# Thirty-eight more idle matmuls ahead of two waits of TensorE

## The chip, the cores and the metric

The kernel runs on one core of one Trainium2 chip. The metric is the time of the whole program in device microseconds (us), as the median of several runs. One further execution was recorded by the hardware profiler; all traces and rows below are of that one execution, and their times count from its first instruction (its span).

The engines are called by short names: PE is TensorE (matmuls; PEld is its weight load), DVE is VectorE, ACT is ScalarE, POOL is GpSimd, and SP is the queue that issues most DMA transfers.

## What is computed

A gated linear recurrence over 768 steps for 4 batches and 8 heads of width 48 is followed by a two-layer network with the SiLU function on the 3072 rows of width 384 that come out of it:

```python
    f = 1.0 / (1.0 + np.exp(-f_logit))
    for t in range(S):
        state = f[:, :, t, :, None] * state + np.einsum('bhd,bhe->bhde', k[:, :, t], v[:, :, t])
        y[:, :, t] = np.einsum('bhd,bhde->bhe', q[:, :, t], state)
    ...
    h = x @ w_in
    g = h * (1.0 / (1.0 + np.exp(-h)))
    return (g @ w_out).astype(np.float32)
```

Here x is y with the heads side by side, w_in is 384 x 2048 and w_out is 2048 x 384.

## The kernel before

**Units.** The 768 steps are cut into 6 chunks of 128, and one chunk of one batch, with all 8 heads, is a unit: 24 units, and two neighbours make a pair. Within a unit the recurrence is done in matrix form. ACT makes the logs of the gates (E and L in the plan, lines 492 and 494); PE sums them along the chunk with a triangular matrix (cs, L565 and L569); ACT takes exponentials of the sums; POOL scales k (ki, L578) and DVE scales q (qg, L582). PE transposes both (tq, L588) and DVE copies them out (L590). PE multiplies them to scores (sc, L599), DVE masks these (at, L603), and PE makes y from scores, v and the carried state (y, L608 and L612). DVE casts y (yc, L616), PE transposes it (yT, L620), and DVE copies it to xT (xc, L622). PE also makes the unit's own contribution to the state (d, L630), which DVE adds (sd, L635 or L637) and POOL scales (su, L641).

**The network.** PE multiplies the columns of w_in with xT (m1, L529, one unit at a time for the first six units: 12 matmuls for each quarter of w_in; mi, L540, for pairs later), ACT applies SiLU into hT (L526, L536), and PE multiplies by w_out (mo, L551). DVE copies the result out and it is stored.

**Weights.** w_in and w_out arrive as four loads each into staging buffers (L505, L510) and are cast to bf16, a quarter at a time (ci and co in the plan, L518 to L520). The four casts of w_in are on POOL, POOL, POOL and DVE; the fourth quarter's, on DVE, is ci 3. In the plan's order PE uses the quarters 1, 2, 3 and then 0. Quarter 0 of w_in is cast by POOL.

**What sets the order.** A planner at build time (`make_tasks`, `schedule`, `planned`) writes every step down as a task with an engine, a duration, a rank, the tasks that it depends on and the buffers that it takes. It simulates the program once, and the order of tasks on each engine is then fixed; at run time each engine goes through its own list and waits on semaphores. SP's list holds the loads, so a load that waits for a buffer holds back all that is behind it.

PE's list in the stretch that matters is: yT of unit 1; cs of unit 3, which waits for the logs of unit 3; sc of unit 2; m1 of units 0, 1 and 0 (36 matmuls in all); y of unit 2; m1 of unit 1; then m1 of unit 0 with quarter 3, which waits for ci 3; yT of unit 2; m1 of unit 1 with quarter 3; d of unit 2; m1 of unit 2; tq of unit 3; m1 of units 0 and 1 with quarter 0; sc of unit 3; three more m1 of unit 2; and then mo.

**Idle matmuls.** `idle` (L386) looks through PE's plan up to 60 us for gaps. In each it finds the accumulator bank that is free for longest, and counts how many matmuls fill `idle_fill` of that stretch, at 0.0565 us each (0.113 for the first gap). The program then issues that many matmuls of a zero tile (`blank`, 128 x 128) into the bank just before the task that ends the gap; nothing reads their results (`warm`, L650 to L652, called at L672). The planner does not count their time. In the kernel before there are nine such groups, of 21, 23, 15, 18, 4, 18, 5, 6 and 2 matmuls. The group of 6 stands ahead of cs of unit 3, and the group of 2 ahead of m1 of unit 0 with quarter 3.

Of the kernel before, what the change touches and what calls it, by code (L numbers as in the profile page):

```python
# [38 lines left out]
    idle_to=60.0,  # L39
    idle_gap=0.2,  # L40
    idle_fill=0.75,
    hold_exp=0,
    hold_silu=1.23,
    keep_exp=161.0,
# [331 lines left out]
def planned(cfg, slots):  # L376

    tasks, T = make_tasks(cfg)
    schedule(tasks, slots, cfg, cfg["margin"])
    fixed = {e: sorted([t for t in tasks if t.eng == e], key=lambda t: (t.start, t.idx)) for e in ENGINES}  # L380
    schedule(tasks, slots, cfg, 0.0, fixed=fixed)
    order = sorted(tasks, key=lambda t: (t.start, t.idx))
    return order, idle(order, slots, cfg)


def idle(order, slots, cfg):  # L386

    held = {s: [] for s in range(slots["mlp"])}
    banks = {}
    for t in order:  # L390
        for x in t.acq + t.use:
            if x.cls == "mlp":
                lo, hi = banks.get(x, (t.start, t.end))
                banks[x] = (min(lo, t.start), max(hi, t.end))
    for x, (lo, hi) in banks.items():
        held[x.slot].append((lo, hi + 0.3))
    out, prev = [], cfg["idle_from"]
    for t in [t for t in order if t.eng == "PE"]:
        lo, hi = prev, t.start - cfg["idle_gap"]
        prev = t.start + t.dur  # L400
        if t.start > cfg["idle_to"]:
            break
        best = (0.0, 0.0, 0)
        for s, spans in held.items():
            a = max([lo] + [e for b, e in spans if b < hi])
            if hi - a > best[0] + 1e-6:
                best = (hi - a, a, s)
        n = int(best[0] * cfg["idle_fill"] / (0.0565 if out else 0.113))
        if n > 0:
            out.append((best[1], best[2], n))  # L410
    return out
# [296 lines left out]
```

## Time and profile before

| what | value |
|---|---|
| median of 4 runs | 189.99 us (188.86 to 190.88) |
| the profiled execution's own time | 191.16 us |
| its span, first to last instruction | 189.4 us |
| mean granted TensorE clock in it | 0.98 of full |
| PE busy | 176.1 us, 93% of the span |
| ACT busy | 131.2 us, 69% |
| DVE busy | 95.9 us, 51% |
| POOL busy | 70.4 us, 37% |
| idle matmuls (L652) | 112 |

The profiled execution is one sample, and its time is not the median's. The busy shares are means over the whole span. PE is busy nearly throughout, except in the opening: its waits there are for the first logs, for the logs of unit 3 and for the cast of the last-used but one quarter of w_in. A granted clock of 1.00 is full speed, 0.50 is half. In a row of the timeline the first number is the start, the second the length, "xN" the number of instructions merged, and the bracket gives the engine's idle time before the row and what ended it. Rows of PE overlap a little, because a matmul is recorded until its result is written (0.219 us for one of 128 columns) while the next has long begun.

### The profile page before, as it was taken

What the parts mean: (1) busy time and instruction counts of PE and PEld (TensorE: products, weight loads), DVE (VectorE), ACT (ScalarE), POOL (GpSimd) and SP (SyncE); (2) the same over time, 40 slices, a digit from 0 to 9 for tenths busy, and PEclk for the clock granted to TensorE, in tenths of its full rate; (3) what the DMA queues carried; (4) which work ended last, traced back from release to release, by engine and by line L of the source; (5) the groups of instructions that cost most, each with busy time, mean ns of one, the idle gap of its engine ahead of it and who ended that gap; (6) DMA issues with size and microseconds to landing.
All of it is one profiled execution on the core that took longest, in us unless ns stands there. A gap on an engine that the chain in (4) does not pass through costs nothing.

```text
span 189.4 us, 4875 instructions
## 1 busy us (share of the span) xinstructions
PE 176.1 (93%) x2005; PEld 141.6 (75%) x2005; DVE 95.9 (51%) x185; ACT 131.2 (69%) x217; POOL 70.4 (37%) x112
## 2 busy tenths in 40 slices
PE   5985669999999999979999999999999999999991
PEld 4974559877787879778787787668788786966960
DVE  4286244346768793473625736875651515251111
ACT  4460743798797898998988798468669996720720
POOL 2344636734555752382570750581152106000000
PEclk9999786999999999999999999999999999999999
DMA  6999999899999999999999489469785775413101
GB/s 120 203 182 279 393 302 360 214 238 234 191 251 197 246 228 212 208 245 188 195 155 248 100 163 225 88 115 214 144 169 130 158 146 114 121 24 104 42 11 72
DMA packets 120389, 34.22 MB, mean 181 GB/s; under 512 B 116128, under 2 KB 117792, under 8 KB 120368
## 3 DMA queue, kind: packets, MB, share of 16 engines
q1 hardware_dynamic: 119664, 31.76, 77.4%
q0 software_dynamic: 704, 2.16, 3.1%
q8 instruction: 15, 0.25, 0.5%
q14 instruction: 6, 0.05, 0.1%
HBM read 25.17 MB, written 4.72 MB: 158 GB/s over the span
## 4 chain that ended last, share of the span: by engine, by line
PE 77%; SPq 8%; DMA 6%; ACT 5%; issue 1%; DVE 1%; ACTq 0%; DVEq 0%
PE mlp L551 31%; PE mlp L540 24%; PE mlp L529 8%; SPq L485 6%; DMA ws<-in_moe_w_in_dram 6%; PE sc L599 3%; PE yd L612 2%; PE yd L608 2%; PE tq L588 2%; PE cs L565 2%; PE yd L630 2%; ACT L677 2%; PE tq L620 1%; ACT hT L536 1%; ACT e L492 1%
## 5 line engine op out<-in xcount | busy, mean ns | idle before, releaser
L551 PE MATMUL mlp<-w_out,hT 128*128 128x384 bf16 x384 | 69.9, 326 | 0.0
L536 ACT ACTIVATE hT<-mlp 128x512 bf16<-128x512 f32 x72 | 41.7, 597 | 17.4 <-PE mlp L540 14.9
L540 PE MATMUL mlp<-xT,w_in 128*128 128x256 bf16 x432 | 51.5, 273 | 1.1 <-ACT hT L536 1.0
L551 PEld LDWEIGHTS <-hT 128*128 128x128 bf16 x384 | 34.8, 97 | 19.5
L540 PEld LDWEIGHTS <-w_in 128*128 128x128 bf16 x432 | 46.3, 114 | 3.2 <-issue 1.3
L578 POOL TENSOR_TENSOR qk<-k,ia 128x384 bf16<-128x384 f32 x24 | 24.0, 999 | 51.7 <-ACT al L576 30.1
L603 DVE TENSOR_TENSOR atm<-sc,triu 128x512 bf16<-128x512 f32 x48 | 30.9, 685 | 21.0 <-PE sc L599 21.0
L677 ACT ACT_TABLE_LOAD x23 | 29.5, 1283 | 0.4
L641 POOL TENSOR_TENSOR st<-sd,al 48x192 bf16<-48x192 f32 x40 | 20.9, 522 | 17.2 <-DVE sd L635 8.7
L529 PE MATMUL mlp<-xT,w_in 128*128 128x128 bf16 x288 | 21.5, 238 | 1.9 <-DVE w_in L520 1.9
L529 PEld LDWEIGHTS <-w_in 128*128 128x128 bf16 x288 | 19.7, 120 | 2.5 <-DVE w_in L520 2.0
L559 DVE COPY o<-mlp 128x384 f32<-128x384 f32 x22 | 12.2, 556 | 18.2 <-PE mlp L551 14.5
L616 DVE CAST yb<-yd 128x384 bf16<-128x384 f32 x24 | 13.3, 554 | 15.9 <-PE yd L612 15.8
L572 ACT ACTIVATE ia<-cs 128x384 f32<-128x384 f32 x24 | 11.7, 489 | 13.7 <-PE cs L569 7.6
L582 DVE TENSOR_TENSOR qk<-q,cs 128x384 bf16<-128x384 f32 x24 | 13.2, 551 | 11.7 <-ACT cs L574 8.4
L526 ACT ACTIVATE hT<-mlp 128x512 bf16<-128x512 f32 x24 | 13.6, 597 | 7.8 <-PE mlp L529 7.4
L492 ACT ACTIVATE e<-f 128x768 f32<-128x768 f32 (+1 forms) x14 | 10.5, 747 | 8.7 <-DMA f<-in_f_logit_dram 8.7
L580 POOL CAST vb<-v 128x384 bf16<-128x384 f32 x24 | 11.6, 503 | 10.6 <-DMA v<-in_v_dram 7.6
L635 DVE TENSOR_TENSOR sd<-yd,st 128x384 f32<-128x384 f32 x16 | 8.9, 555 | 8.3 <-PE yd L630 6.2
L565 PE MATMUL cs<-lf,triu 128*128 128x384 bf16 x24 | 8.0, 332 | 4.5 <-ACT lf L494 4.5
L574 ACT ACTIVATE cs<-cs 128x384 f32<-128x384 f32 x24 | 11.4, 477 | 0.6
L652 PE MATMUL mlp<-blank 128*128 128x128 bf16 x112 | 10.0, 256 | 1.0 <-DVE blank L657 1.0
(43 smaller groups left out, 151.5 us busy)
## 6 DMA issues: line engine op xcount, KB each, us to landing
f<-in_f_logit_dram SPq DMA_DIRECT2D x10, 384.0 KB, 5.8
k<-in_k_dram SPq DMA_DIRECT2D x10, 384.0 KB, 5.8
q<-in_q_dram SPq DMA_DIRECT2D x10, 384.0 KB, 6.1
v<-in_v_dram SPq DMA_DIRECT2D x10, 384.0 KB, 5.3
ws<-in_moe_w_in_dram SPq DMA_DIRECT2D x4, 768.0 KB, 9.5
wt<-in_moe_w_out_dram SPq DMA_DIRECT2D x4, 768.0 KB, 8.1
out_dram<-o SPq DMA_DIRECT2D x13, 192.0 KB, 2.1
out_dram<-o POOLq DMA_DIRECT2D x11, 192.0 KB, 3.9
```

The lines of the kernel that those rows point to most:

```text
L492: nc.scalar.activation(e, at("f", u // 2)[:, i:i + n], AF.Exp, scale=-1.0)
L526: return nc.scalar.activation(at("hT", P)[:, 4 * j:4 * j + 4, i * C:(i + 1) * C], h, AF.Silu)
L529: nc.tensor.matmul(h[:, r, :], w_tile(kk, 4 * j + r), at("xT", P)[:, kk, i * C:(i + 1) * C], start=(kk == 0), stop=(kk == KT - 1))
L536: return nc.scalar.activation(at("hT", P)[:, 2 * j:2 * j + 2, :], h, AF.Silu)
L540: nc.tensor.matmul(h[:, i, :], w_tile(kk, n), at("xT", P)[:, kk, :], start=(kk == 0), stop=(kk == KT - 1))
L551: nc.tensor.matmul(o, at("hT", P)[:, n, i * C:(i + 1) * C], w_rows(n), start=(n % (NT // 2 if half else NT) == 0), stop=(n == NT - 1 or ha ...
L578: nc.gpsimd.tensor_mul(at("qk", u)[:, 1, :, 0:D], at("k", P)[:, i], at("ia", u))
L582: nc.vector.tensor_mul(at("qk", u)[:, 0, :, 0:D], at("q", P)[:, i], at("cs", u)[:, 0:HD].rearrange("p (h d) -> p h d", d=D))
L603: nc.vector.tensor_mul(at("atm", u)[:, r], at("sc", u)[:, r], triu[:, None, :].to_broadcast([C, NP, C]))
L616: nc.vector.tensor_copy(at("yb", u), at("y", u))
L641: nc.gpsimd.tensor_mul(at("st", u)[lo:lo + D, :, r * D:(r + 1) * D], at("sd", u)[lo:lo + D, :, r * D:(r + 1) * D], at("al", u)[lo:lo + D, ...
L677: nc.scalar.preload_act_table_set(SETS[after[t.idx]])
```

## The change

Two groups get more idle matmuls: the one ahead of the task `cs` of unit 3 gets 14 more (20 in place of 6), and the one ahead of the task `m1` of unit 0 with quarter 3 gets 24 more (26 in place of 2). Names of tasks are joined with underscores to look the numbers up. All else, the order on every engine included, stays.

```diff
@@ -39,6 +39,7 @@
     idle_to=60.0,
     idle_gap=0.2,
     idle_fill=0.75,
+    idle_more={'cs_3': 14, 'm1_0_3': 24},
     hold_exp=0,
     hold_silu=1.23,
     keep_exp=161.0,
@@ -406,6 +407,7 @@
             if hi - a > best[0] + 1e-6:
                 best = (hi - a, a, s)
         n = int(best[0] * cfg["idle_fill"] / (0.0565 if out else 0.113))
+        n += cfg["idle_more"].get("_".join(map(str, t.name)), 0) if n else 0
         if n > 0:
             out.append((best[1], best[2], n))
     return out
```

## The prediction

> **What bounds the kernel now.** I read the chain of work that ended last first, because a change on TensorE (PE) pays only where PE is on it. In order of time (start, length, what) it is this around the two places that the change touches:
>
> ```profile
> 15.93 11.04 DMA ws<-in_moe_w_in_dram
> 27.00 0.97 DVE w_in L520
> 28.01 1.35 PE mlp L529 x12
> 29.36 0.32 PE tq L620 x3
> 29.68 1.28 PE mlp L529 x12
> ```
>
> Up to 28.01 us the end is set by a load of w_in and its cast on VectorE (DVE); the first wait, cs of unit 3 at 20.68, is not on the chain. From 28.01 on it is nearly all PE, and the waits of PE from 31 to 186 us come to 1.0 us in all. So time saved on PE before 28.01 is lost again in the wait for the cast; time saved after 28.01 can reach the end. The timeline of PE shows both waits, the idle time in brackets:
>
> ```profile
> 17.12 0.50 PE L652 MATMUL mlp<-blank 128*128 128x128 bf16 x6
> 20.68 0.32 PE L565 MATMUL cs<-lf,triu 128*128 128x384 bf16 x1 [3.06 <-ACT lf L494]
> ...
> 21.34 3.82 PE L529 MATMUL mlp<-xT,w_in 128*128 128x128 bf16 x36
> ...
> 25.88 0.28 PE L652 MATMUL mlp<-blank 128*128 128x128 bf16 x2
> 28.01 1.35 PE L529 MATMUL mlp<-xT,w_in 128*128 128x128 bf16 x12 [1.86 <-DVE w_in L520]
> ...
> 34.22 2.20 PE L529 MATMUL mlp<-xT,w_in 128*128 128x128 bf16 x36
> ```
>
> The 36 matmuls after the first wait take 3.82 us, the same 36 at 34.22 take 2.20. The reason is the clock. I laid windows over the stretch from where the half-us windows change from 1.00 to 0.50 and back (the columns are stretch, length, PE busy with its count, granted clock, DMA share, GB/s):
>
> ```profile
> 14.55:17.96 3.41, 2.44 (x39) 1.00 0.95 276
> 17.96:21.38 3.42, 0.70 (x14) 1.00 1.07 391
> 21.38:24.79 3.41, 3.41 (x35) 0.50 1.08 370
> 24.79:28.20 3.41, 1.55 (x31) 1.00 1.04 293
> 28.20:31.62 3.42, 3.42 (x37) 0.50 0.99 380
> 31.62:35.03 3.41, 3.41 (x63) 1.00 1.05 244
> ```
>
> Twice a stretch of 3.41 us in which PE was little busy (0.70 us, then 1.55 us, 45%) is followed by one at half clock. A stretch with 2.44 us (71%) is followed by full clock. The second half-clock stretch, 28.20 to 31.62, lies on the chain.
>
> **The change part by part.** It adds 38 matmuls of zeros (with 38 weight loads, overlapped) and no wait, transfer or work on another engine. Each is costed from the rows of L652: 18 in 1.18 us at 9.66 us, of which the last takes its full 0.219, so (1.18 - 0.219)/17 = 0.0565 us each at full clock; 21 in 2.42 us at 0.99 us, of which the last takes some 0.31, so 2.11/20 = 0.106 us each at half.
>
> First wait, 14 more: 14 x 0.0565 = 0.79 us, so that the run of 20 ends near 18.4 instead of 17.62. At half clock, 20 x 0.106 = 2.1 us ends at 19.3. Both are hidden by the wait for the logs, which ends at 20.68; cost on the path 0. Cover gone, it would cost 0.79. What it buys: busy time in 17.96 to 21.38 rises from 0.70 to about 1.15 us, 34%. That is under the 45% after which the clock fell, so I expect the half clock from 21.38 to stay. Did it go, PE would reach the second wait about 1.7 us earlier and wait for the cast that much longer: worth nothing by itself.
>
> Second wait, 24 more: 24 x 0.0565 = 1.36 us, because the clock row says 1.00 from 24.79 on. The 26 end near 27.5 and the matmuls of unit 0 behind them start at 28.01 when the cast is done, as before: 0.5 us to spare, cost 0. The other bound is half clock, 25.88 + 26 x 0.106 = 28.64, a delay of 0.63 us; I take 0, since nothing in that stretch ran at half. What it buys: busy time in 24.79 to 28.20 becomes 1.55 + 1.36 = 2.91 us, 85%, above the 71% that kept full clock. So 28.20 to 31.62 should be at full clock.
>
> **Worked out at full clock** (12 matmuls of L529 = 12 x (2.20 - 0.22)/35 = 0.68 us; transposes and d 0.17 each, as their rows in the chain after 39 us have it): m1 of unit 0 from 28.01 to 28.69, yT of unit 2 to 28.86, m1 of unit 1 to 29.54, d to 29.71, m1 of unit 2 to 30.39. Its input xT is ready: the yT that ends at about 29.02 with its tail is copied by DVE in 0.36 us, by 29.41. Next come the transposes tq of unit 3, and here a load is late next:
>
> ```profile
> 30.45 0.56 DVE L582 TENSOR_TENSOR qk<-q,cs 128x384 bf16<-128x384 f32 x1 [0.38 <-DMA q<-in_q_dram]
> ```
>
> That product waits for q of unit 3 until 30.45, not for PE, ends at 31.01, and tq can start at about 31.08. It started at 32.01. So 0.93 us is gained of some 1.6, and 0.7 becomes a wait for q. The next, m1 of unit 0 with the cast on GpSimd (POOL) that ends at 29.72 + 1.46 = 31.18, is ready when tq is done at 31.53.
>
> The gain then has to pass unit 4's q, whose load is queued on SP behind a load of w_out:
>
> ```profile
> 34.65 0.34 SPq L510 DMA_DIRECT2D wt<-in_moe_w_out_dram  x1
> 35.03 1.37 SPq L485 DMA_DIRECT2D k<-in_k_dram  x1
> 36.45 2.67 SPq L485 DMA_DIRECT2D q<-in_q_dram  x1
> ```
>
> ```profile
> 42.87 0.55 DVE L582 TENSOR_TENSOR qk<-q,cs 128x384 bf16<-128x384 f32 x1 [2.25 <-DMA q<-in_q_dram]
> ```
>
> The w_out load waits for a buffer that a POOL cast frees, which follows the state update of unit 2, which follows DVE's sd at 31.37. With PE early, sd comes right behind the product that ends at 31.01, so this train moves 0.35 us at most. The product at 42.87 then ends between 43.07 (the load comes 0.35 earlier) and 43.42 (it lands as before), tq of unit 4 can start 0.07 later, and it started at 43.88: gain left 0.74 or 0.39, by the share of the DMA engines (1.16 on average from 40 to 50 us) rather between them. I take 0.6. Behind it PE waits for no q until 91.75 us, where DVE waited 0.24 for one, and one v at 136 us came late by 7.6 us on POOL without stopping PE; I charge nothing for these, and lower the end of the range for them.
>
> **Sum for the profiled execution:** 0 + 0 - 0.6, a span of 189.4 to about 188.8, and 191.16 to 190.56 in its own time. That execution lies 1.17 above the median of the runs, 189.99, and above the highest, 190.88. It may be one that met both half-clock stretches where others did not.
>
> **A rule that speaks against the change.** TensorE: Matmul & The Clock Gate (its sections on the clock gate and on why it matters) says that the clock drops after an idle window of about 3.4 us, and gives as a rule that only gaps over about 3 us matter. By that rule the second wait, 1.86 us, does no harm and the sum is 0: 189.99. The trace shows half clock after it, so I go by the trace. The same page (section What's actually happening) says that the window runs free and does not start with the kernel; one trace can't show that. If so, the boundaries lie elsewhere in each execution, and the gain of 0.6 belongs only to those where the second wait fills one window. I estimate that most but not all do, and move the median by 0.5.
>
> **Rivals.**
> - *Nothing changes*: 190.0. The median execution has no half clock after 28, or the gain is held up at the late loads of q. For it: 189.99 against 191.16, and the two waits for q. Against it: PE waits only 1.0 us behind 31.
> - *Slower, by the first 14*: if a window's boundary falls into the middle of the first wait, 2.3 us of idle time split in two may no longer lower the clock. Then PE is at full clock at 21.34, reaches the second wait some 1.7 us earlier, at about 24.2, finishes its 26 blanks at 25.7, and idles 2.3 us until 28.01: more than the 1.86 that sufficed. The half clock then comes after 28 in executions that before came to the second wait late and did not have it. Price 0.4 to 0.93, so 190.4 to 190.9. It decides once the boundaries lie about 0.9 to 1.4 us later than in this trace. Against it: with the boundaries of this trace it does not happen.
> - *The blanks are too long*: a cast done 0.5 us earlier than here, or half clock under the blanks, makes them delay unit 0's matmuls by up to 0.63: 190.6 without a gain, but full clock follows and pays that back. I count it into the one before.
>
> **How the numbers follow.** Gain of 0.3 to 1.0 at the median (189.0 to 189.7): 0.5. Nothing: 0.3, at 189.99 and 0.4 to each side, since four runs spread over 2.02. Slower: 0.2, 190.3 to 191.2. The likeliest gives 189.99 - 0.5 = 189.5; its own range is 188.9 to 189.8. For eight times in ten I leave out a tenth at each side: 188.6 to 190.8. A measurement of this kernel tells about 1% from no change, which is 1.9 us here: more than the whole half-clock stretch can cost (1.7). So faster by over 1% has 0.08, which only scatter of the runs adds; slower by over 1% has 0.05; within 1% 0.87.
>
> **What would show it.** Right: 20 and 26 blanks before the two waits, the first wait at about 2.3 us and the second at 0.5, half clock still once near 21 to 25 but full clock from 28 to 32, tq of unit 3 near 31.1 behind a wait of some 0.7 for q, tq of unit 4 near 43.3. Wrong in the step on the clock: a stretch at 0.50 behind 28 all the same. Wrong in the step on the loads: full clock there, and unit 4's tq at 43.5 or later. Wrong in cost: m1 of unit 0 later than the cast's end plus 0.05. A change of over 1.9 us would mean that something other than these two waits has moved.

## The result, and the profile after

The changed kernel takes 189.82 us (median of 36 runs), the kernel before 189.93 (55 runs). The ratio of the two times, changed over before, is 1.0002, with a 95% interval of 0.9989 to 1.0014: no change, within a quarter of a microsecond. Runs in a slower state, here one of the 36 at 194.04 us, are left out of every ratio. The profiled execution of the changed kernel took 190.72 us, its span is 188.95.

The clock did what the change can make it do. In the page of the changed kernel the row of the granted clock, in 40 slices of the span, is never below nine tenths:

```profile
PEclk9999999999999999999999999999999999999999
```

The row says nothing of the opening: the trace records the clock only from its first rise, here at 10.56 us, and the idle matmuls ahead of that go at half pace (23 in 2.61 us).

The timeline of PE around the two waits (lines are two higher after the change: L567 is cs, L531 m1, L590 tq, L654 the idle matmuls, called blanks below):

```profile
18.31 1.28 PE L654 MATMUL mlp<-blank 128*128 128x128 bf16 x20
19.90 0.32 PE L567 MATMUL cs<-lf,triu 128*128 128x384 bf16 x1 [0.31 <-ACT lf L496]
...
24.35 1.61 PE L654 MATMUL mlp<-blank 128*128 128x128 bf16 x26
27.29 0.86 PE L531 MATMUL mlp<-xT,w_in 128*128 128x128 bf16 x12 [1.33 <-DVE w_in L522]
...
30.70 0.62 PE L590 MATMUL tq<-ident,qk 128*128 128x128 bf16 x8 [0.87 <-DVE qk L584]
...
43.22 0.32 PE L567 MATMUL cs<-lf,triu 128*128 128x384 bf16 x1 [0.61 <-DVE qk L584]
43.38 0.24 PE L571 MATMUL cs<-ones,lf 128*128 128x1 bf16 x4
43.48 0.61 PE L590 MATMUL tq<-ident,qk 128*128 128x128 bf16 x8
```

The 20 and 26 blanks cost nothing, and the twelve matmuls of unit 0 at 27.29 run at full clock (0.86 us, where they took 1.35). But two brackets are new. PE waits 0.87 us ahead of tq of unit 3 and 0.61 ahead of cs of unit 5, both for DVE's product of q and the decays. In the kernel before PE came to cs of unit 5 without a wait:

```profile
43.62 0.33 PE L565 MATMUL cs<-lf,triu 128*128 128x384 bf16 x1
...
43.88 0.61 PE L588 MATMUL tq<-ident,qk 128*128 128x128 bf16 x8
```

The chain of work that ended last, after the change, no longer comes through the cast of w_in:

```profile
22.08 7.92 DMA q<-in_q_dram
...
30.09 0.57 DVE qk L584
...
30.70 0.62 PE tq L590 x8
...
42.63 0.55 DVE qk L584
...
43.22 0.32 PE cs L567
...
43.62 0.47 PE tq L590 x8
```

Between 30.70 and 42.63 this chain runs along PE, and the timeline of DVE names a matmul as what ended its wait for the second product:

```profile
42.62 0.56 DVE L584 TENSOR_TENSOR qk<-q,cs 128x384 bf16<-128x384 f32 x1 [3.16 <-PE mlp L553]
```

That is a coincidence: the product reads q and cs, and no result of that matmul. q of unit 4 landed at 42.49 and the product began 0.13 us later, just as in the kernel before (42.74 and 42.87), where the row names the load of q.

From 43.48, the start of tq of unit 4, to the end are 145.46 us; in the kernel before, from 43.88, they are 145.51. Everything that differs between the two executions is decided before that point.

The granted clock is listed for every run. One half-clock stretch of 3.41 us lowers the mean over 188 us by 0.009, and the idle end of the program by at most 0.005; a mean below 0.994 therefore means half clock before the end (no run of the two kernels lies between 0.991 and 0.995). Of the kernel before 67 of 131 runs in the sessions of the experiments have it, of the changed kernel 5 of 36. The mean does not tell behind which wait it came; in the three traces of the kernel before that have it, it came behind the second each time, and in one of them behind the first too. So the change removes the half clock from about two executions in five, and the time stays. The trace that the prediction was built on is of a rare kind: its mean of 0.980 stands for two half-clock stretches, and only 8 of the 131 runs come down to 0.982 or less.

### The profile page after: what moved, and what is told of

Read it like the earlier page. It is cut to its first block, busy times and chain, and to the rows that moved or that the text cites. A ratio compares the mean times of both kernels' runs of the same rounds, so it can differ in the third digit from the quotient of the medians.

```text
span 188.9 us, 4951 instructions
## 1 busy us (share of the span) xinstructions
PE 176.9 (94%) x2043; PEld 141.7 (75%) x2043; DVE 95.8 (51%) x185; ACT 131.2 (69%) x217; POOL 70.5 (37%) x112
## 4 chain that ended last, share of the span: by engine, by line
PE 75%; SPq 11%; ACT 5%; DMA 4%; issue 1%; DVE 1%; DVEq 0%; ACTq 0%
PE mlp L553 32%; PE mlp L542 24%; SPq L487 6%; PE mlp L531 6%; DMA q<-in_q_dram 4%; SPq L507 4%; PE sc L601 3%; PE yd L614 2%; PE yd L610 2%; PE tq L590 2%; PE cs L567 2%; ACT L679 2%; PE yd L632 1%; PE tq L622 1%; ACT hT L538 1%
## 5 line engine op out<-in xcount | busy, mean ns | idle before, releaser
L542 PEld LDWEIGHTS <-w_in 128*128 128x128 bf16 x432 | 46.3, 114 | 3.2 <-issue 1.3
L618 DVE CAST yb<-yd 128x384 bf16<-128x384 f32 x24 | 13.3, 554 | 15.9 <-PE yd L614 15.8
L531 PE MATMUL mlp<-xT,w_in 128*128 128x128 bf16 x288 | 18.7, 220 | 2.0 <-DVE w_in L522 1.3
L531 PEld LDWEIGHTS <-w_in 128*128 128x128 bf16 x288 | 16.8, 114 | 2.8 <-DVE w_in L522 1.5
L654 PE MATMUL mlp<-blank 128*128 128x128 bf16 x150 | 12.9, 256 | 1.0 <-DVE blank L659 1.0
L654 PEld LDWEIGHTS <-blank 128*128 128x128 bf16 x150 | 11.4, 118 | 1.2 <-DVE blank L659 1.0
```

The lines of the kernel that those rows point to most:

```text
L531: nc.tensor.matmul(h[:, r, :], w_tile(kk, 4 * j + r), at("xT", P)[:, kk, i * C:(i + 1) * C], start=(kk == 0), stop=(kk == KT - 1))
L542: nc.tensor.matmul(h[:, i, :], w_tile(kk, n), at("xT", P)[:, kk, :], start=(kk == 0), stop=(kk == KT - 1))
L618: nc.vector.tensor_copy(at("yb", u), at("y", u))
L654: nc.tensor.matmul(buf["mlp", bank][:, 0:C], blank, blank, start=True, stop=True, skip_group_check=True)
```

## The experiments

There are two theories. By the first, PE sets the end from 28 us on: the half clock costs time wherever it comes, and the gain is lost to some cost of the blanks. By the second, the loads of q of units 3 and 4 make PE wait there anyway and swallow most of what the half clock takes. I began with the first ("my theory" in the first two expectations below) and held the second from the kernel with 30 blanks on. A ratio is always to the kernel before; kernels of one session share its runs.

**One part alone: the first wait.**

```diff
-    idle_more={'cs_3': 14, 'm1_0_3': 24},
+    idle_more={'cs_3': 14},
```

> Only the 14 more ahead of cs of unit 3 (20), the second wait keeps its 2. My theory, that the half clock behind the second wait costs time wherever it comes, says: PE reaches the second wait at full clock, near 24.2, and idles 3 us or more before the cast, so nearly every execution has half clock behind 27 to 28; tq of unit 3 near 32 in place of 30.7, the time 0.4 to 0.9 us above the kernel before where that does not have it, 190.3 to 190.8. The rival, that loads of q hold the work behind it and the clock there is hidden, says: within 0.2 of the kernel before.

Measured: ratio to the kernel before 1.0004 (0.9981 to 1.0027), 189.57 us. Half clock came in only 2 of 14 runs, where I had expected it in nearly every one, so this time does not decide between the theories. Its windows, laid in steps of 3.41 us from where its trace has the clock first rise (8.44 us), show why:

```profile
22.09:25.50 3.41, 2.19 (x38) 1.00 1.10 359
25.50:28.92 3.42, 2.11 (x39) 1.00 1.10 358
```

The second wait is 2.27 us long here, longer than the 1.86 that lowered the clock before, but a boundary cuts it in two, and each half keeps PE busy for more than 2 us.

**The other part alone: the second wait.**

```diff
-    idle_more={'cs_3': 14, 'm1_0_3': 24},
+    idle_more={'m1_0_3': 24},
```

> Only the 24 more ahead of m1 of unit 0 with quarter 3 (26), the first wait keeps its 6. My theory: the clock can still fall in the first wait, as before, which costs nothing because the cast comes later; it stays full behind the second wait in nearly every execution; the time is that of the changed kernel or up to 0.3 below the kernel before, 189.6 to 189.9. If half clock in the first wait reaches into the stretch behind it, or the 26 blanks at half clock delay m1 of unit 0, 0.3 to 0.6 above.

Measured: 1.0008 (0.9987 to 1.0028), 189.44 us, half clock in 2 of 14 runs. As expected of the clock behind the second wait; no gain in time either. Neither part hides a loss of the other.

**PE made late ahead of the stretch.**

```diff
-    idle_more={'cs_3': 14, 'm1_0_3': 24},
+    idle_more={'cs_3': 14, 'm1_0_3': 100},
```

> 100 more in place of 24 ahead of m1 of unit 0 with quarter 3 (102 in all, 5.8 us at full clock), so that PE comes to that task about 2.8 us after the cast. It measures how much of a delay of PE there reaches the end. With the waits for q of unit 3 (0.87 us of PE in the trace of after) and of unit 4 (0.61) as slack: 1.2 to 1.4 us above the changed kernel, about 191.1. If PE alone sets the end from 28 on: 2.8 above, 192.6. If loads set it: 0 to 0.3 above.

Measured: 1.0128 (1.0097 to 1.0160), 192.09 us, 2.4 us above the changed kernel by the ratios. By its interval the delay is 1.8 to 3.0 us; that leaves out the 1.2 to 1.4 of the slack and takes in the 2.8 of PE alone, so by its time this kernel (six runs) speaks for the first theory. The trace offers another way: PE's delay also delays the load of q. DVE's sd of unit 2, POOL's state update and the w_out cast behind it come late, and the buffer for the next load of w_out is freed late. These are POOL and SP in that trace:

```profile
31.60 1.08 POOL L643 TENSOR_TENSOR st<-sd,al 48x192 bf16<-48x192 f32 x2 [2.24 <-DVE sd L639]
32.75 2.88 POOL L522 CAST w_out<-wt 128x1536 bf16<-128x1536 f32 x2
```

```profile
34.24 0.34 SPq L512 DMA_DIRECT2D wt<-in_moe_w_out_dram  x1
34.63 0.96 SPq L487 DMA_DIRECT2D k<-in_k_dram  x1
35.63 3.14 SPq L487 DMA_DIRECT2D q<-in_q_dram  x1
```

The w_out load goes out 9.9 us after quarter 3 of w_in has landed (24.34), against 7.6 in the changed kernel, and q of unit 4 lands 17.9 us after it, against 16.2. Another 0.8 us is lost behind the landing (the span ends 147.23 after it, against 146.46), where DVE's copy of a result waits 0.85 us for a store at 49.91 and PE 0.49 for DVE at 50.78. Together 2.5 us; PE had come 3.7 us late to unit 0 (29.03, the cast done at 25.32), so some 1.2 were swallowed here too. That is one trace.

**PE made late behind the wait, by somewhat more than the half clock takes.** 30 blanks between d of unit 2 and m1 of unit 2:

```diff
         if n > 0:
             out.append((best[1], best[2], n))
+        if t.name == ("m1", 2, 1):
+            out.append((t.start, t.acq[0].slot, 30))
```

> The changed kernel with 30 more idle matmuls, 1.7 us at full clock, behind the wait for the cast: ahead of m1 of unit 2, between d of unit 2 and tq of unit 3. They stand in for what the half clock costs there, without the clock. If the loads of q of units 3 and 4 set the time and the half clock only eats PE's waits for them (0.75 and 0.2 to 0.6 us in the traces): 0.3 to 0.7 us above the changed kernel. If PE sets the end from 28 us on: 1.7 above.

Measured: 1.0031 (1.0009 to 1.0052), 190.33 us: about 0.55 us above the changed kernel by the ratios, as the second theory has it, and well under 1.7. In its trace the wait ahead of tq of unit 3 is gone and the one ahead of cs of unit 5 is still there:

```profile
28.68 1.84 PE L656 MATMUL mlp<-blank 128*128 128x128 bf16 x30
30.36 0.83 PE L533 MATMUL mlp<-xT,w_in 128*128 128x128 bf16 x12
31.02 0.61 PE L592 MATMUL tq<-ident,qk 128*128 128x128 bf16 x8
```

```profile
43.33 0.32 PE L569 MATMUL cs<-lf,triu 128*128 128x384 bf16 x1 [0.53 <-DVE qk L586]
```

In this one execution the 1.7 us cost nothing behind the landing of q of unit 4 (42.59). But that q landed 16.7 us after quarter 3 of w_in, later than without the 30 blanks (15.5 to 16.2), and one trace can't tell whether the blanks did that. The runs as a whole say that they cost something.

**The load ahead of q held up by a buffer.** The last load of w_out gets a staging buffer of w_in that has long been free, all orders kept:

```diff
     fixed = {e: sorted([t for t in tasks if t.eng == e], key=lambda t: (t.start, t.idx)) for e in ENGINES}
+    T["wo", 2].acq[0].cls = "ws"
...
     at = lambda *key: where[key]
+    where["wt", 2] = where["wt", 2].rearrange("p k n -> p (k n)").rearrange("p (a d) -> p a d", d=d_model)
```

> The changed kernel, with the third load of w_out in the order of loads for the longest wait (wo 2) landing in a staging buffer of w_in that is long free, in place of the one of w_out that the cast of POOL frees at 33.8; all orders and the numbers of blanks stay. k and q of unit 4 behind it on SP then go out some 4 us earlier. If the wait for q of unit 4 is what held the gain back: PE's wait of 0.61 us at cs of unit 5 is gone, and the time falls by 0.6, to about 189.2. If the gain is lost elsewhere, or the earlier loads delay those of w_out and v of unit 3: 0 to 0.3 above the changed kernel.

Measured: 1.0016 (0.9993 to 1.0039), 189.77 us: no gain. But k and q went out only 0.5 us earlier than in the trace of the changed kernel, not 4, so the run does not test what an early q is worth. SP in its trace:

```profile
26.81 1.90 SPq L489 DMA_DIRECT2D f<-in_f_logit_dram  x1
28.80 5.40 SPq L514 DMA_DIRECT2D ws<-in_moe_w_out_dram  x1
34.24 0.43 SPq L489 DMA_DIRECT2D k<-in_k_dram  x1
34.72 3.57 SPq L489 DMA_DIRECT2D q<-in_q_dram  x1
```

The cast that it waits for was done at 19.13 (the one that reads this buffer before it in the plan; the profile infers a later cast of POOL), and yet the issue takes from 28.80 to 34.20, until the transfers ahead of it are nearly through (the fourth quarter of w_out landed at 33.91). With the buffer free, SP's queue itself holds the load back, and q of unit 4 landed 15.9 us after quarter 3 of w_in, within the 15.5 to 16.2 of the kernel before, the changed one and its two parts. So freeing the buffer alone does not bring q forward.

**The late q taken away.** The same load is left out, in the kernel before, in the changed one, and in the changed one with the 30 blanks:

```diff
-            if t not in first:
+            if t not in first and t.name != ("wo", 2):
                 emit(t)
```

> The kernel before without the load of one quarter of w_out (wo 2, 768 KB, ahead of k and q of unit 4 on SP); its cast reads what the buffer holds, so a quarter of w_out is wrong. It takes away the late q of unit 4. If that load is what hides the half clock, this kernel still has half clock in some two executions of five and those are 0.7 to 0.9 us longer than its others, so that it lies 0.3 to 0.5 above the changed kernel without that load. If the clock is without effect, the two are within 0.15.

> The changed kernel without the load of that quarter of w_out (wrong in the same quarter). PE's wait ahead of cs of unit 5 is gone, 0.2 to 0.6 us in the traces, so 0.2 to 0.6 below the changed kernel, 189.0 to 189.4. If something other than q of unit 4 sets the time there, as it would be if POOL or ACT did: no change.

> The changed kernel without that quarter of w_out and with the 30 idle matmuls of the stand-in. Only the wait for q of unit 3, 0.75 us, is left to hide them: 0.9 to 1.0 us above the kernel without the load alone. If another wait hides them: less than 0.4; if none does: 1.7.

Measured: 1.0014 (0.9992 to 1.0037), 0.9984 (0.9965 to 1.0003) and 1.0022 (0.9997 to 1.0047); medians 189.58, 189.51 and 190.15 us; half clock in 11 of 22, 2 of 22 and 0 of 14 runs. By the ratios the changed kernel gains some 0.3 us by it, as expected, though the intervals with and without the load overlap. Its trace shows the wait ahead of cs of unit 5 gone, and the one for q of unit 3 still there:

```profile
30.45 0.62 PE L590 MATMUL tq<-ident,qk 128*128 128x128 bf16 x8 [0.86 <-DVE qk L584]
...
42.30 0.33 PE L567 MATMUL cs<-lf,triu 128*128 128x384 bf16 x1
42.47 0.24 PE L571 MATMUL cs<-ones,lf 128*128 128x1 bf16 x4
42.57 0.61 PE L590 MATMUL tq<-ident,qk 128*128 128x128 bf16 x8
```

In the three traces the span ends 158.32, 158.37 and 158.39 us after q of unit 3 has landed (at 29.05, 29.75 and 28.60): with the later load out of the way, the earlier one sets the time. With that load in place it is 158.4 to 159.4, the 100 blanks aside, so there was at most 1 us to win.

Between the first two kernels the change is worth 0.0030 of the time by the ratios, 0.57 us, where it was worth nothing with the late load; but the intervals overlap and the medians differ by 0.07 only. The 30 blanks cost 0.7 us, somewhat under the 0.9 to 1.0 expected. Both go the way of the second theory. Against it, the kernel before is no faster without the load (1.0014; the interval leaves a gain of 0.15 us), where its runs at full clock should gain. The times of these three are an indication, no more.

**A second queue for that load.** It is issued from ACT, behind the SiLU of m1 of unit 2 (staging buffer as above):

```diff
-            if t not in first:
+            if t not in first and t.name != ("wo", 2):
                 emit(t)
+            if t.name == ("s1", 2, 1):
+                emit(next(x for x in tasks if x.name == ("wo", 2)))
...
-            return nc.sync.dma_start(out=dst[:, 0] if w == 4 else dst, in_=src[:, 0] if w == 4 else src)
+            return (nc.scalar if m == 2 else nc.sync).dma_start(out=dst[:, 0] if w == 4 else dst, in_=src[:, 0] if w == 4 else src)
```

> The changed kernel with the held-up load of w_out (wo 2) issued from ACT's queue, behind the SiLU of m1 of unit 2, into a staging buffer of w_in that is free by then. SP goes straight from f to k of unit 4. If what sets the time is the landing of q of unit 4, and that is late because SP's queue takes nothing new from 29 to 33 us while the DMA engines run dry near 34, q lands 0.5 to 1.5 us earlier and the kernel is 0.3 to 0.6 below the changed one, 189.0 to 189.3. If the load on the second queue only delays w_out's other quarter and v of unit 3, or q still lands when the bytes ahead of it have: no change or up to 0.5 above.

Measured: 1.0047 (1.0026 to 1.0068), 191.01 us, slower by some 0.85 than the changed kernel. The DMA engines no longer run dry (414 GB/s from 34 to 35 us, where the changed kernel has 57). But SP is held up all the same, now at k:

```profile
28.97 7.25 SPq L489 DMA_DIRECT2D k<-in_k_dram  x1
```

q of unit 4 lands 15.5 us after quarter 3, 0.7 less than in the changed kernel's trace but no less than in that of the first wait alone. And v of unit 3 now lands at 36.44 in place of 34.89, so that PE has a new wait of 0.87 us, about what the kernel loses, and then comes to cs of unit 5 late enough not to wait there:

```profile
37.06 0.36 PE L616 MATMUL yd<-vb,atm 128*128 128x48 bf16 x8 [0.87 <-POOL vb L584]
```

**The kernel before, three more traces.** No edit.

> The kernel before once more, for its trace. In the five traces in which PE waits for q of unit 4, the span is the landing of that q plus 146.45 to 146.48 us. My theory says that this holds here too, half clock or not, within 0.3: the half clock behind the second wait costs 0 to 0.3. If the half clock costs what it takes from PE, an execution with it is the landing plus 147 or more.

> The kernel before once more, for another trace: as for the one ahead of it, the span is the landing of q of unit 4 plus 146.45 to 146.75, with or without half clock behind 27 us; plus 147 or more with half clock if that costs its full length.

> The kernel before a third time, for another trace: the span is the landing of q of unit 4 plus 146.45 to 146.75, with or without half clock behind 27 us; plus 147 or more with half clock if that costs its full length.

Measured, beside the other traces with that load on SP (us from each span's start; landings as the traces record them):

| trace | half clock behind the second wait | q of unit 4 landed | PE's wait at cs of unit 5 | span | span less landing |
|---|---|---|---|---|---|
| before | 28.21 to 31.62 | 42.74 | 0 | 189.39 | 146.65 |
| before, a | 28.15 to 31.56 | 41.65 | 0 | 188.30 | 146.65 |
| before, b | none | 41.17 | 0.59 | 187.67 | 146.50 |
| before, c | 26.78 to 30.19 | 41.60 | 0 | 188.10 | 146.50 |
| changed | none | 42.49 | 0.61 | 188.95 | 146.46 |
| first wait alone | none | 41.31 | 0.17 | 187.79 | 146.48 |
| second wait alone | none | 41.41 | 0.25 | 187.87 | 146.46 |
| free staging buffer | none | 41.90 | 0.48 | 188.34 | 146.44 |
| 30 blanks behind | none | 42.59 | 0.53 | 189.05 | 146.46 |
| 100 more blanks ahead | none | 42.27 | 0 | 189.50 | 147.23 |

All but the last, the kernel with 100 more blanks, end 146.44 to 146.65 us after q of unit 4 has landed; 147 or more would have meant that the half clock costs its full length. Half clock adds 0 to 0.2. The landings themselves differ by 1.6 us between the four executions of the kernel before. Trace c (timeline of PE) shows half clock that costs nothing at all: PE loses time from 26.78 on, and comes to cs of unit 5 just as it may start.

```profile
26.68 1.43 PE L529 MATMUL mlp<-xT,w_in 128*128 128x128 bf16 x12 [2.69 <-DVE w_in L520]
...
28.22 1.49 PE L529 MATMUL mlp<-xT,w_in 128*128 128x128 bf16 x12
...
42.34 0.32 PE L565 MATMUL cs<-lf,triu 128*128 128x384 bf16 x1
```

## Why the prediction was right, and where it was not

**No change within 1%: right,** and little risked by it: by the prediction's own sum a whole half-clock stretch costs at most 1.7 us, under 1% of the time. The measured 189.82 us lies in the range given, 0.3 above the likeliest value.

**The step on the clock** held in its outcome: half clock became rare (5 of 36 runs against 67 of 131). The picture drawn for it did not come. In the changed trace the clock first rose at 10.56 us in place of 7.73, and PE came to the first blanks 1.2 us later (18.31 against 17.12); the waits left behind the blanks are 0.31 and 1.33 us, not 2.3 and 0.5, and the half clock expected from 21 to 25 us is not there.

**The blanks' own cost** was 0, as summed. In six of the seven traces with 26 blanks before the second wait, 1.0 to 1.8 us of wait is left behind them. In the seventh, without the w_out load and with the 30 blanks behind, the cast was done early, at 25.43, and no wait is left; yet unit 0's matmuls start at 25.48, the same 0.05 us after the cast as elsewhere.

**The gain of 0.5 us: not there.** The step that failed is the passage to unit 4, "gain left 0.74 or 0.39 ... I take 0.6". Two things were wrong in it.

- I let tq of unit 4 follow DVE's product directly, "0.07 later". In PE's list cs of unit 5 stands between them, and it waits for the same product, which frees its accumulator bank. From the product's end to tq are 0.30 us (43.18 to 43.48 after the change), not 0.07. In the kernel before the product ended at 43.42 and tq started at 43.88, so 0.15 us was to be had where I counted 0.39.
- I let the load of q move 0.35 us with the state update. The traces do not show that: q of unit 4 lands 15.8 to 16.0 us after quarter 3 of w_in in the three with half clock, 15.5 to 16.2 in those of the kernel before, the changed one and its parts without it, and freeing the buffer does not bring it forward. Longer delays of PE may move it: 16.7 us with the 30 blanks, 17.9 with the 100.

Together that leaves 0 to 0.2 us for an execution with half clock. The same can be read from PE alone. From m1 of unit 0 (27.29) to cs of unit 5 (43.22) the changed kernel has 15.93 us less waits of 0.87 and 0.61, that is 14.45 of work; the three traces with half clock have 15.61 to 15.66. So the half clock takes 1.2 us from PE, and the waits for q of units 3 and 4 together are 0.9 to 1.5 us in the full-clock traces of the kernel before, of the changed one and of its two parts. One replaces the other.

**The estimate that most executions have the half clock** was high: about half do. With 0 to 0.2 us in two executions of five that are cured, the median should move by less than 0.1; 0.04 the wrong way, with an interval of a quarter either way, agrees.

**The rivals.** "Nothing changes" is what happened, by the cause it named: the gain is held up at the late loads of q. "Slower, by the first 14" did not come: the kernel with those alone is no slower, and has half clock in 2 of 14 runs only. "The blanks are too long" did not come either, by the seven traces above; it took 76 more of them to make PE late.

**The rule that spoke against the change** gave the right time for another reason. The Trainium skill (TensorE: Matmul & The Clock Gate, section Why this matters for your kernels) lets gaps under about 3 us pass, and here gaps of 1.86 to 2.93 us were followed by half clock; it is the load behind, not a clock kept full, that made this free.

**What stays open.** In the kernel before, runs with one half-clock stretch are 0.6 to 0.9 us longer than those without (medians 189.88 against 188.97, 189.81 against 189.13, 190.20 against 189.61 in three sessions). The half clock can't be the cause of most of it by the traces above. Nor by the change itself: taken from two executions in five, 0.6 to 0.9 us would be a gain of 0.2 to 0.3, and the interval leaves at most 0.2. Late loads would explain both, since a later cast makes the wait longer and the clock fall, and q late as well; four traces of that kernel agree with it, but four are few, and no run here fixed the loads. Nor do the traces show what share of executions pays for the 30 blanks, and no experiment brought q of unit 4 forward without taking a load away, so what an earlier q is worth is not shown.

## What to carry to other kernels

Before counting a gain on PE, follow it to the next input that PE does not make itself, and list every instruction of PE's queue between that input and the point where you read the gain: the one that waits first decides. A wait that shows as zero on PE can be slack of a load that only just came in time, so compare when the load landed with when PE used it. And where the time follows one landing from execution to execution (here to 0.2 us), look at that transfer first.

## What the runs showed of the hardware that was not expected

- The clock followed how busy PE was in a fixed stretch of 3.41 us, not the length of a gap alone: a gap of 1.86 us lowered it, and one of 2.27 us that a boundary cut in two did not. From the first rise to 45 us, stretches with PE busy for 0.70, 0.72, 1.25 and 1.55 us were followed by half clock; those with 1.70 us (the kernel before without the w_out load), 1.82 (30 blanks) and more were not. These two are from the kernel before (trace a and trace b):

```profile
24.74:28.15 3.41, 1.25 (x22) 1.00 1.10 351
```

```profile
23.72:27.13 3.41, 1.91 (x39) 1.00 1.07 332
```

The recorded busy time does not order all of them: near the end of the kernel with the first wait alone, a stretch with 1.46 us (182.52 to 185.93) was not followed by half clock. An exact threshold is not shown.

- Where the boundaries lie differs between executions, which one trace could not show: the clock first rose at 7.67, 7.73, 9.71 and 10.07 us in the four traces of the kernel before.
- An issue on SP's queue took 5.4 us with nothing that its semaphores still had to wait for, while earlier transfers were in the queue; with that load on ACT's queue, the k next on SP took 7.25 us.
